# Attention feeding a mixture of experts on one core: tiles placed ahead of the gate products, constant matmuls moved, and weight splits placed later

## The chip, the core and the metric

The kernel runs on one core of a Trainium2 chip. Five engines work side by side, each through its own queue in order: TensorE (PE, with PEld for its weight loads), VectorE (DVE), ScalarE (ACT), GpSimd (POOL) and SyncE (SP), which only issues transfers. The metric is the device time of one launch in microseconds.

## The reference

The reference is two stages in float32. The first is linear attention over 8 batches, 8 heads, 576 positions and a head width of 64, with a norm per head:

```python
kv = np.einsum('bhsd,bhse->bhde', k, v)
out = np.einsum('bhsd,bhde->bhse', q, kv)
rms = np.sqrt(np.mean(out * out, axis=-1, keepdims=True) + 1e-06)
x = (out / rms * g_norm)          # 4608 tokens of 512 columns
```

The second routes every token to one of 8 experts and applies that expert's two matrices:

```python
logits = x @ w_gate;  e_idx = np.argmax(logits, axis=1)
gate_w = softmax(logits)[e_idx];  eom = sigmoid(x @ w_output_gate)
for e in range(8):
    h = np.maximum(x[e_idx == e] @ w1[e], 0.0)        # 512 -> 1024
    out[e_idx == e] = gate_w * eom[:, e] * (h @ w2[e])  # 1024 -> 512
```

## The kernel before

The program has two stages that overlap. **The attention stage** (`p1_main`, L870) goes batch by batch. `kv_part` multiplies keys with values (PSUM tile kvps, L504; copied to aug by ScalarE at L510 and to kvc by VectorE at L512). `kvT_part` transposes the result (kvTps, L521; ScalarE's copy to kvT, L523). `m_part` forms the gate products, so that logits come out of the same matmul as the attention rows (mps, L534; ScalarE's copy into aug, L536). `out_tile` (ops, L574) then makes one tile of 128 tokens from the queries and aug; it uses one of the two PSUM buffers tagged "big", as do mps and the later hps, and ScalarE empties it in three steps (L579 rows, L581 squares, L582 gate products). In batch b the tiles of batch b-1 are worked, four or five of them. The text calls the stretch from one kvps to the next a half-loop.

Every tile also advances the routing of finished groups of tiles (8, 8, 8 and 12 tiles; `route`, L605): VectorE sums squares (L595), norms, takes the maximum, counts with TensorE (rps, L709 to L716), and makes one-hot tiles la (L752; by GpSimd in the first two groups, by a mixture in the others) and rrc (L762 to L769). TensorE sums these into a table of row numbers (tblps, L782), from which VectorE makes the gather list gidx (L942 for the lead, L953 for the rest). A group's weights and norms go out as xtail (L775, written by L804).

**The expert stage** works on runs. After 24 tiles the fullest expert's first 384 tokens are taken as the *lead*, run 0; run 1 is that expert's remainder; runs 2 to 8 are the other experts. A run gathers its rows (xg, L244), scales heads (L260), transposes (tps, L284, in PSUM buffers tagged "t", emptied by L289 and L290 into a high and a low part), multiplies with the first weights (hps, L322; 3 matmuls per product of high and low parts; hT by L337 and L338) and then with the second (yps, L371). Weights arrive raw (wraw, L199) and `split` makes the high and low part: L219 on ScalarE and L222 on VectorE for the first weights, L226 and L229 for the second.

On TensorE, ScalarE, VectorE and GpSimd the order in this stage is the order in which the code is written. Two things set it. `HOOKS` and `TAIL` are strings of steps: R advances the routing, L takes a step of the lead (`lead_run`, L390), S makes one split of the lead's second weights (`lead_w2`, L405). `COLD` counts *constants* (`constant`, L482): matmuls of a tile of ones whose result nobody reads. They stand in kvps (two per piece for the first three batches), in kvTps (2), in mps (3), and as three of 512 columns after each `m_part` (cps). SP's order is set by a scheduler.

Of the kernel before, what the change touches and what calls it, by code (L numbers as in the profile page):

```python
# [69 lines left out]


HOOKS = {15: 'R', 27: 'RR', 28: 'R', 31: 'RGW', 32: 'X', 34: 'NL'}
TAIL = "QLLLLRRRSLSRRSLLRRRLSLRRSRLSLL"

WAITS = {}

# [7 lines left out]


COLD_B = 3
COLD = (2, 20, 2, 3, 3)

ROUND = 1.5 * 2.0 ** 30

# [39 lines left out]
def tiles_of(i):  # L130

    _, t0, n = RUNS[i]
    return [(t0 + k, k * P, min(P, n - k * P)) for k in range(-(-n // P))]
# [6 lines left out]
def body(ctx: ExitStack, tc: tile.TileContext, kvm, rem, qT, wg, gn, w1, w2, kc, xs, tab, out):  # L140
# [249 lines left out]
    def lead_run():  # L390

        split(0, 1, 0, SPLITS[0])
        yield
        for k in range(len(tiles_of(0))):
            stage(0, k)
            yield
        split(0, 1, 1, SPLITS[1])
        yield
        for f in range(8):
            mm1(0, f)  # L400
            if f in (0, 2):
                split(0, 1, f // 2 + 2, SPLITS[f // 2 + 2])
            yield
# [78 lines left out]
    def constant(ps, n, start=True):  # L482

        for _ in range(n):
            k = ps.shape[1] // P
            nc.tensor.matmul(ps, ones, ones.unsqueeze(1).to_broadcast([P, k, P]), start=start, stop=start)

    def kv_part(b):

# [58 lines left out]
    def out_tile(g):  # L548
# [9 lines left out]
            chunk[:] = [g, take([P, 2, DM], F32, "xrow")]  # L558
        xrow = chunk[1][:, g - chunk[0]]
        ps = ps_b.tile([P, 2, 512], F32, name="ops", tag="big")  # L560
        parts = []
        n0 = g * P
        while n0 < (g + 1) * P:
# [41 lines left out]
    def route(gi):  # L605
# [171 lines left out]
        if gi == LEAD_GROUP:  # L777
            lead_placed.append(gi)
        yield from pause(8)
        for t in range(n):  # L780
            g = g0 + t
            nc.tensor.matmul(tps, las[t], rc[:, t, 0:2], start=(g in (0, LEAD_TILES)), stop=(g in (LEAD_TILES - 1, NT - 1)))  # L782
# [87 lines left out]
    def p1_main():  # L870
        load(SPARE)
        for b in range(B):
            lim = tiles_ready(b - 1) if b else 0
            cp = kv_part(b)
            load(SPARE)
            run_out(lim)
            kvT = kvT_part(cp)
            run_out(lim)
            run_out(lim)
            m_part(b, kvT)  # L880
            constant(ps_t.tile([P, 512], F32, name="cps", tag="t"), COLD[4])
            while done_tiles < lim:
                run_out(lim)
        while done_tiles < NT:
            run_out(NT)
        for step in TAIL:
            act(step)
        while routing:
            advance()
# [321 lines left out]
```

## Time and profile before

| | us |
|---|---|
| median of 3 runs | 588.94 |
| lowest, highest | 587.86, 590.38 |
| profiled execution, whole | 591.15 |
| its span | 589.4 |
| TensorE busy | 562.4 (95%) |
| VectorE busy | 258.3 (44%) |
| mean granted clock | 0.963 |

The busy shares are averages over both stages. In the timeline a row is start, duration, engine, line, operation and tiles with the count of merged instructions, and in brackets the idle time before it with what ended that. A matmul's duration includes its passage through the array; starts of successive rows give the rate. In rows of stretches the columns are the stretch, its length, busy time and count for PE, PEld, DVE, ACT and POOL, then the granted clock (1.00 is full), the share of the transfer engines, and GB/s.

### The profile page before, as it was taken

How to read it: one execution, taken by the hardware profiler on the slowest of the kernel's cores; microseconds unless marked ns; L12 is line 12 of the kernel's file. 1: busy time of each engine (PE TensorE's matmuls, PEld its weight loads, DVE VectorE, ACT ScalarE, POOL GpSimd, SP SyncE). 2: the span in 40 equal slices, each digit the busy share in tenths (PEclk: the TensorE clock that was granted, in tenths of full speed). 3: DMA queues.
4: the chain of work that ended last, by engine and by line, in shares of the span. 5: the costliest groups of instructions: out<-in, count | busy, mean ns of one | idle time of the engine just before them, and what ended most of it. 6: DMA issues, size and time to landing. Idle time of an engine off the chain costs nothing.

```text
span 589.4 us, 10666 instructions
## 1 busy us (share of the span) xinstructions
PE 562.4 (95%) x4287; PEld 491.6 (83%) x4287; DVE 258.3 (44%) x562; ACT 223.2 (38%) x411; POOL 145.8 (25%) x150
## 2 busy tenths in 40 slices
PE   7999898869999999999999999999999999999995
PEld 4677777758798998889889987998799889889974
DVE  2136677698325556325531443244334424523410
ACT  1356555643235334323432343235234323532410
POOL 2002330401722511620172027003600540011011
PEclk9899898578999999999999999999999999999998
DMA  8999995681564622342335233524342343200001
GB/s 277 382 408 405 408 374 173 225 295 32 156 254 135 213 78 92 107 159 85 123 95 185 80 108 99 175 72 132 101 153 100 111 165 103 80 36 20 1 19 45
DMA packets 33460, 92.26 MB, mean 157 GB/s; under 512 B 8801, under 2 KB 8929, under 8 KB 33408
## 3 DMA queue, kind: packets, MB, share of 16 engines
q1 hardware_dynamic: 26672, 71.63, 34.5%
q0 software_dynamic: 6304, 19.70, 10.6%
q8 instruction: 35, 0.57, 0.4%
q10 hardware_dynamic: 432, 0.21, 0.1%
q14 instruction: 17, 0.14, 0.1%
HBM read 72.34 MB, written 19.70 MB: 156 GB/s over the span
## 4 chain that ended last, share of the span: by engine, by line
PE 79%; DMA 7%; issue 5%; DVE 4%; POOL 2%; ACT 1%; POOLq 0%; SPq 0%; DVEq 0%
PE hps L322 35%; PE yps L371 33%; PE yps L365 3%; PE tps L284 3%; DMA ld<-qT 2%; PE ops L574 2%; DMA ld<-rem 2%; PE kvps L504 2%; POOL la L752 2%; DMA ld<-kvm 2%; DMA xg<-xs,gidx 1%; DVE ss L595 1%; DMA out<-y,oidx 0%; DVE wlo L222 0%; DVE wlo L229 0%
## 5 line engine op out<-in xcount | busy, mean ns | idle before, releaser
L322 PE MATMUL hps<-xT,whi 128*128 128x256 f32 (+8 forms) x1024 | 192.7, 306 | 5.1 <-DVE hT L338 4.6
L371 PE MATMUL yps<-whi,hT 128*128 128x512 f32 (+3 forms) x592 | 195.0, 398 | 0.0
L322 PEld LDWEIGHTS hps<-xT,whi 128*128 128x128 f32 x1024 | 160.1, 191 | 7.2 <-DVE hT L338 4.2
L371 PEld LDWEIGHTS yps<-whi,hT 128*128 128x128 f32 (+3 forms) x592 | 110.1, 186 | 24.1
L322 PE MATMUL hps<-xT,wlo 128*128 128x304 f32 (+8 forms) x512 | 119.6, 305 | 0.0
L371 PE MATMUL yps<-wlo,hT 128*128 128x512 f32 (+3 forms) x296 | 115.9, 392 | 0.0
L338 DVE SCALAR_TENSOR_TENSOR hT<-hps,hT 128x512 fp32r<-128x512 f32 (+6 forms) x112 | 57.9, 518 | 124.3 <-ACT hT L337 124.3
L337 ACT ACTIVATE hT<-hps 128x512 fp32r<-128x512 f32 (+6 forms) x112 | 51.5, 460 | 144.8 <-PE hps L322 115.0
L322 PEld LDWEIGHTS hps<-xT,wlo 128*128 128x128 f32 x512 | 87.4, 191 | 0.0
L244 POOL DMA_INDIRECT xg<-xs,gidx x42 | 42.7, 1018 | 169.3 <-PE tps L284 91.8
L382 POOL DMA_INDIRECT out<-y,oidx x42 | 44.5, 1059 | 147.9 <-ACT y L381 106.6
L371 PEld LDWEIGHTS yps<-wlo,hT 128*128 128x128 f32 (+3 forms) x296 | 55.1, 186 | 11.2
L222 DVE SCALAR_TENSOR_TENSOR wlo<-wraw,gcol,whi 128x1024 fp32r<-128x1024 f32 x32 | 44.4, 1387 | 40.2 <-ACT whi L219 40.2
L381 ACT ACTIVATE y<-yps,tl 128x512 f32<-128x512 f32 (+3 forms) x37 | 25.5, 688 | 71.4 <-PE yps L371 67.6
L260 POOL TENSOR_TENSOR xg<-xg 128x512 f32<-128x512 f32 (+7 forms) x39 | 41.7, 1072 | 41.0 <-DMA xg<-xs,gidx 33.9
L289 ACT CAST xT<-tps 128x512 fp32r<-128x512 f32 (+9 forms) x45 | 23.2, 518 | 68.7 <-PE tps L284 67.1
L290 DVE TENSOR_TENSOR xT<-tps,xT 128x512 fp32r<-128x512 f32 (+9 forms) x45 | 27.1, 604 | 44.5 <-ACT xT L289 44.0
L229 DVE TENSOR_TENSOR wlo<-wraw,whi 128x1024 fp32r<-128x1024 f32 x32 | 39.2, 1224 | 14.2 <-ACT whi L226 7.1
L574 PE MATMUL ops<-aug,ld 64*128 64x80 f32 (+1 forms) x640 | 41.8, 289 | 0.6 <-issue 0.6
L574 PEld LDWEIGHTS ops<-aug,ld 64*128 64x128 f32 (+1 forms) x640 | 37.3, 194 | 5.8 <-ACT aug L536 3.0
L219 ACT ACTIVATE whi<-wraw,gcol 128x1024 fp32r<-128x1024 f32 x31 | 35.5, 1145 | 0.0
L226 ACT CAST whi<-wraw 128x1024 fp32r<-128x1024 f32 x32 | 33.3, 1041 | 1.7 <-DMA wraw<-w 1.7
(163 smaller groups left out, 400.6 us busy)
## 6 DMA issues: line engine op xcount, KB each, us to landing
wraw<-w SPq DMA_DIRECT2D x64, 512.0 KB, 3.6
ld<-kvm SPq DMA_DIRECT2D x32, 512.0 KB, 10.1
ld<-qT SPq DMA_DIRECT2D x18, 512.0 KB, 10.2
xs<-xrow SPq DMA_DIRECT2D x13, 512.0 KB, 11.6
xs<-xrow SPq DMA_DIRECT2D x2, 1280.0 KB, 15.0
ld<-rem SPq DMA_DIRECT2D x3, 512.0 KB, 10.2
xg<-xs,gidx POOLq DMA_INDIRECT x42, 3.6
out<-y,oidx POOLq DMA_INDIRECT x42, 3.1
```

The costliest lines, as they stand in the source:

```text
L219: he.activation(hi, r, AF.Copy, scale=gcol[:, 0:1])
L222: eng.scalar_tensor_tensor(out=lo, in0=r, scalar=gcol[:, 0:1], in1=hi.bitcast(F32), op0=ALU.mult, op1=ALU.subtract)
L226: he.copy(hi, r)
L229: eng.tensor_tensor(out=lo, in0=r, in1=hi.bitcast(F32), op=ALU.subtract)
L244: gathered = nc.gpsimd.indirect_dma_start(out=x[:M, :], out_offset=None, in_=rows, in_offset=bass.IndirectOffsetOnAxis(ap=gidx[:M, p, t:t ...
L260: eng.tensor_tensor(out=v, in0=v, in1=f, op=ALU.mult)
L322: nc.tensor.matmul(ps[:, j, :n], w[:, o:o + P], x[d][:, j * N:j * N + n], start=(d == 0 and k == 0), stop=(d == 3 and k == 2))
L337: nc.scalar.activation(hh, x, AF.Relu)
L338: nc.vector.scalar_tensor_tensor(out=v(h[:, l:l + n]), in0=x, scalar=0.0, in1=hh.bitcast(F32), op0=ALU.max, op1=ALU.subtract)
L371: nc.tensor.matmul(ps[:M], a, b, start=(f == 0 and k == 0), stop=(f == 7 and k == 2))
L382: i_ = nc.gpsimd.indirect_dma_start(out=out, out_offset=bass.IndirectOffsetOnAxis(ap=oidx[:M, p, t:t + 1], axis=0), in_=y[:M], in_offset=N ...
L574: nc.tensor.matmul(ps[r0:r0 + m, u, p * W:(p + 1) * W], qt[g // 2][r, p, q0:q0 + m], augs[b % 3][r, p, :], start=True, stop=True)
```

## The change

Four edits are made. In each batch but the first, two tiles now stand ahead of `kvT_part` and all other tiles of the previous batch between it and `m_part`; before it was one tile and two tiles, with the rest behind `m_part`. In the last batch one tile stays ahead of `kvT_part`, one stands between, and two come behind `m_part`. The constants in kvTps go from 2 to 1, in mps from 3 to 1, and the three of 512 columns after `m_part` go. New constants stand in the late tiles (from tile 28 on, two of 192 columns each, in a part of the tile's PSUM that the tile does not use), ahead of the lead group's table (five of 512) and ahead of each of the lead's three transposes (four of 512, in a buffer tagged "t"). And in `TAIL` the first S steps move behind later routing and lead steps, and two S at the end of the list of splits go, since there are only four splits.

```diff
-TAIL = "QLLLLRRRSLSRRSLLRRRLSLRRSRLSLL"
+TAIL = "QLLLLRRRLRRLLRRRSLSLRRSRLSLL"
...
-COLD = (2, 20, 2, 3, 3)
+COLD = (2, 20, 1, 1)
+COLD_L = (2, 5, 4)
+COLD_TILES = 28
...
         for k in range(len(tiles_of(0))):
+            constant(cold(), COLD_L[2])
             stage(0, k)
...
-            k = ps.shape[1] // P
-            nc.tensor.matmul(ps, ones, ones.unsqueeze(1).to_broadcast([P, k, P]), start=start, stop=start)
+            k = ps.shape[1] // D
+            nc.tensor.matmul(ps, ones, ones[:, 0:D].unsqueeze(1).to_broadcast([P, k, D]), start=start, stop=start)
+    def cold():
+        return ps_t.tile([P, 512], F32, name="cps", tag="t")
...
         ps = ps_b.tile([P, 2, 512], F32, name="ops", tag="big")
+        if g >= COLD_TILES:
+            constant(ps[:, 1, NP * W:512], COLD_L[0])
...
         yield from pause(8)
+        if gi == LEAD_GROUP:
+            constant(cold(), COLD_L[1])
...
             run_out(lim)
+            if b + 1 < B:
+                run_out(lim)
             kvT = kvT_part(cp)
-            run_out(lim)
-            run_out(lim)
+            while done_tiles < (lim if b + 1 < B else lim - 2):
+                run_out(lim)
             m_part(b, kvT)
-            constant(ps_t.tile([P, 512], F32, name="cps", tag="t"), COLD[4])
             while done_tiles < lim:
                 run_out(lim)
```

Line numbers after the change are 4 to 13 higher than before. How the instructions stand on TensorE in the half-loop of batch 5 (its kvps starts at 65.01 us before); repeated rows are left out. Before:

```order
L504 MATMUL kvps<-ld 64x64 x40
L574 MATMUL ops<-aug_116,ld 128x80 x8
L486 MATMUL kvTps<-ones 128x256
...
L521 MATMUL kvTps<-ident,kvc 128x128 x2
L574 MATMUL ops<-aug_116,ld 128x80 x16
L486 MATMUL mps<-ones 128x256
...
L534 MATMUL mps<-gw,kvT 64x16 x8
L486 MATMUL cps<-ones 128x512
...
L574 MATMUL ops<-aug_116,ld 128x80 x8
L504 MATMUL kvps<-ld 64x64 x40
```

and now:

```order
L511 MATMUL kvps<-ld 64x64 x40
L583 MATMUL ops<-aug_116,ld 128x80 x16
L490 LDWEIGHTS ones
L490 MATMUL kvTps<-ones 128x256
L528 MATMUL kvTps<-ident,kvc 128x128 x2
L583 MATMUL ops<-aug_116,ld 128x80 x16
L490 MATMUL mps<-ones 128x256
L541 MATMUL mps<-gw,kvT 64x16 x8
L511 MATMUL kvps<-ld 64x64 x40
```

One tile is eight rows of ops: two tiles now stand ahead of the transposes and two behind, the gate products come directly ahead of the next kvps, and cps is gone. On VectorE, from the last gate scaling of the last group to its third hT; before:

```order
L229 TENSOR_TENSOR wlo<-wraw,whi 128x1024
L338 SCALAR_TENSOR_TENSOR hT<-hps,hT 128x384
L222 SCALAR_TENSOR_TENSOR wlo<-wraw,gcol,whi 128x1024
L229 TENSOR_TENSOR wlo<-wraw,whi 128x1024
L655 TENSOR_REDUCE lg<-gp 128x12x8
...
L681 TENSOR_TENSOR ohb_120<-rsc,rsx 128x96
L229 TENSOR_TENSOR wlo<-wraw,whi 128x1024
L338 SCALAR_TENSOR_TENSOR hT<-hps,hT 128x384 x2
```

and now:

```order
L341 SCALAR_TENSOR_TENSOR hT<-hps,hT 128x384
L225 SCALAR_TENSOR_TENSOR wlo<-wraw,gcol,whi 128x1024
L664 TENSOR_REDUCE lg<-gp 128x12x8
...
L690 TENSOR_TENSOR ohb_120<-rsc,rsx 128x96
L341 SCALAR_TENSOR_TENSOR hT<-hps,hT 128x384 x2
```

Three splits of the second weights have left this place. They now stand behind the last group's table, ahead of the gather list of run 1 (VectorE, now):

```order
L784 TENSOR_TENSOR xtail<-rdn 128x12
L937 TENSOR_TENSOR t_2029<-tblps,perm 128x96
...
L941 SCALAR_TENSOR_TENSOR gl<-t_2031 128x6
L232 TENSOR_TENSOR wlo<-wraw,whi 128x1024
L341 SCALAR_TENSOR_TENSOR hT<-hps,hT 128x384
...
L965 TENSOR_TENSOR gif<-gif,gl 128x3
L969 TENSOR_TENSOR tbl<-tbl,tla 128x48
L341 SCALAR_TENSOR_TENSOR hT<-hps,hT 128x384
L966 CAST gidx<-gif 128x3
```

Between the third hT and the list there is nothing else; the left-out rows in the middle are the second and third split and the second hT. On TensorE the table's matmuls (tblps) of the last group stood behind nine yps and now stand ahead of them. On SP the lead's xtail write now stands ahead of the lead's first weight load, where it stood behind it.

## The prediction

> **What bounds the kernel now.** I read the page first, then the chain of waits, then the timelines of the engines between 30 and 150 us.
>
> ```profile
> span 589.4 us, 10666 instructions
> PE 562.4 (95%) x4287; PEld 491.6 (83%) x4287; DVE 258.3 (44%) x562; ACT 223.2 (38%) x411; POOL 145.8 (25%) x150
> ```
> ```profile
> 143.80 3.37 DMA xg<-xs,gidx
> 147.19 0.69 DVE xg L260
> ...
> 147.96 0.64 PE tps L284 x4
> ...
> 157.12 7.03 PE yps L371 x30
> 164.14 13.74 PE hps L322 x96
> 177.89 2.08 PE yps L371 x9
> 179.97 0.44 PE tps L284 x4
> ```
> The second fence is the chain of waits. From the first transposes of the remainder run (tps at 147.96) it is TensorE alone, matmul after matmul, to the last tiles. So nothing behind that point changes, and the whole question is **when tps(147.96) starts**: whatever moves it moves the end by as much. It waits for a gather whose list comes from the routing of the last group. Before it lie the attention half-loops, one per batch. Their TensorE rows:
>
> ```profile
> 41.73 2.70 PE L504 MATMUL kvps<-ld 128*64 128x64 f32 x80
> ...
> 51.60 2.63 PE L504 MATMUL kvps<-ld 128*64 128x64 f32 x77
> ...
> 65.01 3.83 PE L504 MATMUL kvps<-ld 128*64 128x64 f32 x80
> ...
> 72.96 0.49 PE L486 MATMUL mps<-ones 128*128 128x256 bf16 x3 [0.46 <-ACT gp L582]
> ...
> 73.73 0.82 PE L486 MATMUL cps<-ones 128*128 128x512 bf16 x3
> 74.48 1.12 PE L574 MATMUL ops<-aug,ld 64*128 64x80 f32 x16
> 75.54 2.63 PE L504 MATMUL kvps<-ld 128*64 128x64 f32 x77
> ...
> 87.69 4.21 PE L504 MATMUL kvps<-ld 128*64 128x64 f32 x80
> ```
> A half-loop runs from one kvps row to the next. Two of them (from 51.60 and from 75.54) hold a wait for GpSimd, which makes eight one-hot tiles one after the other:
>
> ```profile
> 58.21 5.16 POOL L752 TENSOR_SCALAR la<-ni,rlon 128x128 bf16<-128x128 f32 x8 [9.10 <-DVE rlon L731]
> 81.56 4.88 POOL L752 TENSOR_SCALAR la<-ni,rlon 128x128 bf16<-128x128 f32 x8 [18.18 <-DVE rlon L731]
> ```
> These end at 63.37 and 86.44; TensorE stands behind them in order. The others are paced by TensorE and ScalarE.
>
> **Part 1: constants out of the half-loops, tiles ahead of the gate products.** Each half-loop loses three 128x512 constants (0.75 us, from 73.73 to 74.48) and three of 128x256 (0.14 each by the row at 72.96, 0.42), so 1.17 us. The stall of 0.46 there does not vanish: the gate products now wait for the PSUM of a later tile. ScalarE's pace sets that:
>
> ```profile
> 71.08 0.46 ACT L523 COPY kvT<-kvTps 128x256 f32<-128x256 f32 x1
> 71.54 0.58 ACT L579 COPY xrow<-ops 128x512 f32<-128x512 f32 x1
> ...
> 72.68 0.66 ACT L579 COPY xrow<-ops 128x512 f32<-128x512 f32 x1
> ```
> One tile takes it 1.14. With four tiles, kvps is free to start again after one tile on TensorE (1.06, 74.48 to 75.54), three on ScalarE (3.42), its kvT copy (0.4) and the gate products (0.45): 5.3 us after the last kvps ended. Before it was 6.7 (68.84 to 75.54). A plain half-loop therefore gains **1.4**. Two lie ahead of the first GpSimd wait, and that would be 2.8, unless the loads are later:
>
> ```profile
> 34.92 4.23 SPq L479 DMA_DIRECT2D ld<-kvm x4
> 40.09 0.33 SPq L479 DMA_DIRECT2D ld<-rem x1
> ...
> ld<-rem SPq DMA_DIRECT2D x3, 512.0 KB, 10.2
> ```
> The remainder rows issued at 40.09 land 10.2 later, at 50.3, and the last fifth of kvps (0.5) can end at 50.8, where it ended at 54.2. So 3.4 is the most, and 2.8 fits. In the half-loop from 51.60 the chain kvps, VectorE, GpSimd has a fixed length, and behind it now stand a tile and the gate products (0.45) where there was a tile: 0.4 is given back. The half-loop from 65.01 gains 1.4, and the one from 75.54 gives back 0.4 again. The kvps at 87.69 starts 2.8 - 0.4 + 1.4 - 0.4 = **3.4 earlier**. Bounds: 0, if each half-loop only waits longer for the loads or GpSimd, and 5.0, if the last kvps also runs at the warm 2.63 instead of 4.21.
>
> **Part 2: constants ahead of the lead.** From the last kvps the path is VectorE's routing of the lead group, the gather, GpSimd's scaling and the transposes:
>
> ```profile
> 92.35 0.42 DVE L512 COPY kvc<-kvps 128x256 f32<-128x256 f32 x1 [2.11 <-ACT aug L510]
> ...
> 101.43 0.17 DVE L775 TENSOR_TENSOR xtail<-rdn 128x8 f32<-128x8 f32 x1
> ```
> ```profile
> 100.63 0.88 PE L782 MATMUL tblps<-rrc,la 128*128 128x96 bf16 x8 [1.67 <-DVE rrc L769]
> 101.44 8.27 PE L574 MATMUL ops<-aug,ld 64*64 64x80 f32 x96
> 110.34 2.11 PE L284 MATMUL tps<-ident,xg 128*128 128x128 f32 x8 [0.63 <-POOL xg L260]
> 113.45 1.09 PE L284 MATMUL tps<-ident,xg 128*128 128x128 f32 x4 [0.99 <-POOL xg L260]
> ```
> VectorE works 9.1 us without a gap and its order there is unchanged, so this shifts whole. The five new constants (0.25 each, 1.25) fit into the 1.67 in which TensorE waits. The sixteen of 192 columns (at most 0.14 each, two per tile, 0.28) lie beside ScalarE's 1.14 per tile: nothing; without that cover they would cost 2.2. What they may buy is the clock:
>
> ```profile
> 98.30:101.70 3.40, 1.73 (x33) 1.34 (x34) 3.37 (x16) 1.37 (x3) 0.00 (x0) 1.00 0.44 128
> 101.70:105.10 3.40, 3.40 (x56) 3.23 (x49) 3.04 (x11) 1.90 (x5) 0.29 (x1) 0.50 0.25 51
> ```
> The next to last but one number is the granted clock: after a stretch with the 1.67 gap it fell from 1.00 to 0.50, and the four transposes of 113.45 took 1.09 where 0.44 is the warm figure (179.97). Warm, the two groups of four constants between the transposes (2.0) end as the third tile's rows come: 110.34 + 0.44 + 1.0 + 0.44 + 1.0 = 113.2. Then the part **gains 0.65**. Cold, at twice the time, 110.34 + 1.1 + 2.0 + 1.1 + 2.0 = 116.5, and it **loses 3.1**. I take 0.4 gained, since the constants themselves fill the time in which the clock would come back.
>
> The Trainium skill (TensorE: Matmul & The Clock Gate, "Why this matters for your kernels") lets TensorE fall back only over idle gaps of more than about 3 us. By that rule the 1.67 gap would have been harmless and these constants buy nothing, so the sum below would be 3.9 and the time 585.0 us; the trace, with 0.50 granted behind that gap, disagrees.
>
> **Part 3: the second weights' splits later.**
>
> ```profile
> 122.36 1.22 DVE L229 TENSOR_TENSOR wlo<-wraw,whi 128x1024 fp32r<-128x1024 f32 x1
> 123.50 0.55 DVE L338 SCALAR_TENSOR_TENSOR hT<-hps,hT 128x384 fp32r<-128x384 f32 x1
> ...
> 138.19 0.27 DVE L752 TENSOR_SCALAR la<-ni,rlon 128x128 bf16<-128x128 f32 x1
> ...
> 142.89 0.16 DVE L953 CAST gidx<-gif 128x3 int32<-128x3 f32 x1
> ```
> ```profile
> 124.10 0.61 PE L322 MATMUL hps<-xT,whi 128*128 128x384 f32 x2 [2.88 <-DVE hT L338]
> 139.21 0.68 PE L782 MATMUL tblps<-rrc,la 128*128 128x96 bf16 x12
> ```
> ```profile
> 116.90:138.50 21.60, 16.49 (x77) 15.30 (x77) 20.84 (x55) 10.57 (x20) 0.00 (x0) 0.72 0.60 219
> ```
> The last fence groups VectorE's work (its third pair of numbers): it is busy for 20.84 of 21.60 us and sets the last group's routing. Three splits of 1.2 (122.36) leave that stretch, so the last one-hot tile, done at 138.46, comes 3.6 earlier. The table's matmuls (139.21) no longer stand behind nine yps: another 0.75. That is 4.35 gained up to the table's end (139.9). From there to the list (142.89) it was 3.0. Now the table's five small steps (0.2 each, as the list's 0.16), three splits (3.6), three hT (0.5 each by the row at 123.50) and two list steps (0.4) come first, 6.5: 3.5 is given back. TensorE is no cover there, since hps waits for hT, and the first yps now wait for the first of these splits. Net **0.85 gained**, of which I take 0.5, because cold hps behind the wait at 124.10 can hold back the third hT. Bounds: 0, if it does so fully, and 1.5, if the warm lead brings hT sooner.
>
> **Sum.** 3.4 + 0.4 + 0.5 = 4.3. The span 589.4 becomes 585.1. The profiled execution took 591.15 in all, the median of the three runs is 588.94, 0.5 below the span; the same 4.3 off it gives **584.6 us**.
>
> **Rivals.**
> *Slower: the half-loops go cold.* The constants taken out also kept the clock up. If it stays at 0.50 there, a kvps takes 4.21 instead of 2.63, on three more of them 4.8, and a tile 1.38 (8.27 for 96 matmuls, 16 a tile) instead of 1.06, some seventeen tiles 5.4. Against: rows 41.73 and 51.60 are warm with no constant inside. 10.2 lost against 4.3 gained: 594.8. It turns the sign once the three kvps and no tile are cold (4.8).
> *The lead's constants run cold* (the 116.5 above): part 2 is +3.1 instead of -0.4, 588.1. For it: TensorE still idles ahead of tps until GpSimd is done.
> *The half-loops only wait longer* for loads and GpSimd: part 1 is 0, 588.0. Against: loads landed well ahead from 51.60 on.
> *More than I count*: the clock stays up through the last kvps (1.6) and part 3 reaches 1.5: 582.0.
>
> **Chances.** The forecast 0.50 (its own range 582.8 to 586.5), half-loops cold 0.10, lead's constants cold 0.15, only waiting 0.12, more 0.13. The range that leaves out two in ten runs from 580.8 to 589.5. A measurement of this kernel tells about 0.5%, 2.9 us, from no change: faster than 586.0 is most of the forecast, the last rival and a little of the two in between, 0.60; within 0.5% 0.30; slower 0.10.
>
> **What would show it.** Part 1: the last kvps (87.69) starts near 84.3, and the plain half-loops are about 8 us from kvps to kvps with 2.6 inside. Part 2: a granted clock of 1.00 where 101.70 to 118 had 0.50, and the last four transposes in 0.44. Part 3: the table's matmuls end near 132, the list follows 6.5 later, and tps (147.96) starts near 143.7. A clock of 0.50 in more of the stretch from 20 to 85 us, or tps later than 147, makes the forecast wrong.

## The result, and the profile after

The changed kernel takes 597.91 us (median of 4 runs, 594.71 to 599.08); the kernel before beside it took 589.63 (587.86 to 590.38). The ratio is 1.0125, 95% interval 1.0088 to 1.0161: **1.25% slower**, where 584.6 us had been forecast. The profiled execution took 599.08 us; the head of its page:

```profile
span 597.3 us, 10632 instructions
PE 562.4 (94%) x4272; PEld 491.4 (82%) x4272; DVE 258.5 (43%) x562; ACT 222.2 (37%) x411; POOL 146.5 (25%) x150
```

TensorE is busy for the same 562.4 us, in a span that is 7.9 longer. That the sum is the same says little: in it the tiles' matmuls grew from 41.8 to 43.8 us and kvps from 27.2 to 29.8, while the constants shrank from 24.5 to 22.2 and hps from 312.3 to 308.9. The chain of waits is TensorE alone from the run's first transposes on, as before, so the place to look at is again the start of those transposes:

```profile
150.12 4.36 DMA xg<-xs,gidx
...
155.25 0.66 PE tps L287 x4
```

They start at 155.25 where they started at 147.96, 7.3 later. TensorE's timeline of the half-loops (start, duration, engine, line, operation and tiles, in brackets the idle time before):

```profile
40.57 2.70 PE L511 MATMUL kvps<-ld 128*64 128x64 f32 x80
...
49.02 2.63 PE L511 MATMUL kvps<-ld 128*64 128x64 f32 x77
...
57.57 0.60 PE L793 MATMUL tblps<-rrc,la 128*128 128x96 bf16 x3 [1.47 <-DVE rrc L778]
...
60.86 0.26 PE L793 MATMUL tblps<-rrc,la 128*128 128x96 bf16 x1 [0.32 <-POOL la L761]
61.05 2.00 PE L583 MATMUL ops<-aug,ld 64*128 64x80 f32 x16
...
63.87 4.73 PE L511 MATMUL kvps<-ld 128*64 128x64 f32 x80
68.53 3.70 PE L583 MATMUL ops<-aug,ld 64*128 64x80 f32 x32
...
77.44 3.48 PE L511 MATMUL kvps<-ld 128*64 128x64 f32 x77
...
89.50 0.22 PE L793 MATMUL tblps<-rrc,la 128*128 128x96 bf16 x1 [0.38 <-POOL la L761]
...
92.46 4.43 PE L511 MATMUL kvps<-ld 128*64 128x64 f32 x80
```

Up to the first GpSimd wait all went as forecast: the kvps of batch 4 starts at 49.02 (before 51.60). Then a tile takes 2.00 where a warm one takes 1.12, kvps 4.73, two tiles 3.70, and the last kvps starts at 92.46, 4.8 later than before (87.69). In all the traces here, behind the first 25 us, the granted clock stays at 0.50 for 3.41 us or a multiple of it (before, 64.15 to 67.56); the text calls a stretch of this length a window. The clock in windows (the third number from the right; the first pair of numbers behind the length is TensorE's busy time and count):

```profile
55.45:58.87 3.42, 1.33 (x16) 0.88 (x14) 3.31 (x12) 2.35 (x6) 3.24 (x5) 1.00 1.02 405
58.87:62.28 3.41, 2.20 (x16) 1.64 (x16) 2.75 (x10) 0.00 (x0) 1.94 (x4) 0.50 1.04 413
62.28:65.69 3.41, 3.41 (x59) 3.00 (x59) 0.00 (x0) 1.43 (x4) 0.00 (x0) 0.50 1.01 401
...
75.93:79.35 3.42, 3.42 (x61) 3.02 (x61) 1.54 (x6) 1.84 (x6) 0.00 (x0) 0.50 1.05 386
```

In the wait for GpSimd, TensorE is busy for 1.33 of 3.42 us; then 0.50 is granted for six windows, the last five of which (the first and the last of these are shown) are busy without a gap. Before, only one window behind this wait was at 0.50 (64.15 to 67.56).

Further on, the lead's transposes, and VectorE from the last group's table to the list:

```profile
118.32 1.02 PE L490 MATMUL cps<-ones 128*128 128x512 bf16 x4 [1.20 <-DVE tl L283]
119.45 0.63 PE L287 MATMUL tps<-ident,xg 128*128 128x128 f32 x4
120.54 0.90 PE L325 MATMUL hps<-xT,whi 128*128 128x384 f32 x2 [0.46 <-ACT xT L292]
...
139.75 1.24 PE L793 MATMUL tblps<-rrc,la 128*128 128x96 bf16 x12 [2.81 <-DVE rrc L778]
```
```profile
141.75 1.22 DVE L232 TENSOR_TENSOR wlo<-wraw,whi 128x1024 fp32r<-128x1024 f32 x1
...
148.74 0.56 DVE L341 SCALAR_TENSOR_TENSOR hT<-hps,hT 128x384 fp32r<-128x384 f32 x1 [2.37 <-ACT hT L340]
149.21 0.16 DVE L966 CAST gidx<-gif 128x3 int32<-128x3 f32 x1
```

So the 7.3 us add up by place: +4.8 at the last kvps, +0.8 more up to the lead's first hps (120.54 against 115.00), 4.4 back up to the table's end (140.99 against 139.89), 5.2 lost again up to the list (149.21 against 142.89), and 1.0 in the gather (4.36 against 3.37); the 0.1 that this is too much is rounding.

### The profile page after: what moved, and what is told of

Same layout as the page of the kernel before. It is cut to its first block, busy times and chain, and to the rows that moved or that the text cites. A ratio compares the mean times of both kernels' runs of the same rounds, so it can differ in the third digit from the quotient of the medians.

```text
span 597.3 us, 10632 instructions
## 1 busy us (share of the span) xinstructions
PE 562.4 (94%) x4272; PEld 491.4 (82%) x4272; DVE 258.5 (43%) x562; ACT 222.2 (37%) x411; POOL 146.5 (25%) x150
## 3 DMA queue, kind: packets, MB, share of 16 engines
q0 software_dynamic: 6304, 19.70, 10.5%
## 4 chain that ended last, share of the span: by engine, by line
PE 80%; DMA 7%; DVE 4%; ACT 2%; POOL 2%; issue 2%; SPq 0%; POOLq 0%; DVEq 0%; ACTq 0%
PE hps L325 34%; PE yps L374 32%; PE ops L583 4%; PE yps L368 3%; PE kvps L511 3%; PE tps L287 3%; DMA ld<-qT 2%; DMA ld<-rem 2%; POOL la L761 2%; DMA ld<-kvm 2%; DMA wraw<-w 1%; ACT sq L590 1%; DMA xg<-xs,gidx 1%; ACT xrow L588 1%; DVE wlo L225 1%
## 5 line engine op out<-in xcount | busy, mean ns | idle before, releaser
L325 PE MATMUL hps<-xT,whi 128*128 128x256 f32 (+8 forms) x1024 | 190.5, 303 | 3.7 <-DVE hT L341 3.3
L325 PEld LDWEIGHTS hps<-xT,whi 128*128 128x128 f32 x1024 | 158.4, 189 | 5.7 <-DVE hT L341 3.6
L325 PE MATMUL hps<-xT,wlo 128*128 128x304 f32 (+8 forms) x512 | 118.4, 303 | 0.0
L225 DVE SCALAR_TENSOR_TENSOR wlo<-wraw,gcol,whi 128x1024 fp32r<-128x1024 f32 x32 | 44.5, 1390 | 40.2 <-ACT whi L222 40.1
L293 DVE TENSOR_TENSOR xT<-tps,xT 128x512 fp32r<-128x512 f32 (+9 forms) x45 | 27.2, 605 | 46.1 <-ACT xT L292 44.7
L583 PE MATMUL ops<-aug,ld 64*128 64x80 f32 (+1 forms) x640 | 43.8, 294 | 0.9 <-ACT gp L591 0.4
L583 PEld LDWEIGHTS ops<-aug,ld 64*128 64x128 f32 (+1 forms) x640 | 38.8, 200 | 5.0 <-ACT gp L591 2.4
L511 PEld LDWEIGHTS kvps<-ld 128*64 128x64 f32 (+1 forms) x640 | 26.5, 169 | 9.6 <-DMA ld<-kvm 5.9
```

Of the source, the lines that this page charges most:

```text
L225: eng.scalar_tensor_tensor(out=lo, in0=r, scalar=gcol[:, 0:1], in1=hi.bitcast(F32), op0=ALU.mult, op1=ALU.subtract)
L325: nc.tensor.matmul(ps[:, j, :n], w[:, o:o + P], x[d][:, j * N:j * N + n], start=(d == 0 and k == 0), stop=(d == 3 and k == 2))
L511: nc.tensor.matmul(ps[u * D:(u + 1) * D, p * D:(p + 1) * D], k, v, start=(s == 0 and p == 0), stop=(s == 4 and p == NP - 1))
L583: nc.tensor.matmul(ps[r0:r0 + m, u, p * W:(p + 1) * W], qt[g // 2][r, p, q0:q0 + m], augs[b % 3][r, p, :], start=True, stop=True)
```

## The experiments

All times below are medians, each beside the kernel before on the same chip (590.84 for experiments 1 to 4, 590.49 for 5 to 8, 590.08 for 9 to 11, 590.55 for 12 and 13; the table has them in this order). The right-hand columns come from each run's profile, in us from the start of its span, and show where in the program a run gains or loses: the starts of the last kvps, of the lead's gather list, of the list of run 1, and of that run's first transposes (tps). They are of one execution each: experiments 3 and 4 have the half-loops of before, and their last kvps stands at 87.74 and 86.77.

| run | us | ratio, 95% interval | last kvps | lead's list | list | tps |
|---|---|---|---|---|---|---|
| before | | | 87.69 | 102.88 | 142.89 | 147.96 |
| changed | 597.91 | 1.0125, 1.0088 to 1.0161 | 92.46 | 108.03 | 149.21 | 155.25 |
| constants back | 600.96 | 1.0170, 1.0141 to 1.0198 | 94.75 | 109.87 | 150.81 | 157.35 |
| constants out alone | 597.82 | 1.0135, 1.0099 to 1.0171 | 91.15 | 106.33 | 145.44 | 150.54 |
| splits later alone | 592.09 | 1.0022, 1.0005 to 1.0039 | 87.74 | 101.43 | 142.07 | 148.22 |
| lead's constants alone | 591.78 | 1.0020, 0.9998 to 1.0042 | 86.77 | 101.72 | 141.22 | 146.36 |
| order alone | 600.93 | 1.0185, 1.0138 to 1.0233 | 94.39 | 109.30 | 148.66 | 153.69 |
| order, not at the waits | 591.76 | 1.0011, 0.9985 to 1.0037 | 87.50 | 102.58 | 141.68 | 146.68 |
| changed, waits filled | 591.39 | 1.0008, 0.9983 to 1.0034 | 83.55 | 97.37 | 141.82 | 147.93 |
| early half-loops only | 593.69 | 1.0042, 1.0015 to 1.0070 | 87.21 | 102.17 | 142.87 | 147.95 |
| filled, old splits | 590.69 | 1.0006, 0.9982 to 1.0029 | 84.06 | 99.41 | 141.92 | 146.91 |
| before, waits filled | 590.15 | 1.0002, 0.9978 to 1.0026 | 86.99 | 100.66 | 141.24 | 146.34 |
| filled, no constants at the lead's tps | 589.28 | 1.0000, 0.9976 to 1.0024 | 84.54 | 98.22 | 138.86 | 143.98 |
| the same, splits on GpSimd | 590.88 | 1.0003, 0.9986 to 1.0021 | 84.20 | 98.68 | 141.61 | 146.66 |
| changed, old order at the waits | 595.08 | 1.0078, 1.0051 to 1.0105 | 87.17 | 101.64 | 145.75 | 151.76 |

One thing has to be known to read the last column. From tps to the end of the span it is 441.2 to 442.4 us in ten of the fifteen profiles, and 444.1 to 445.8 in the other five (experiments 5, 6, 8, 9 and 10). In these five the run's second transposes start 5.0 behind the first, and in the ten 2.7 to 3.2. None of the edits is made behind tps; what happens there, the section on the hardware shows. A profile of the five is therefore some 2 to 4 us longer than its tps says.

**1. The constants put back.** The changed kernel, with:

```diff
-COLD = (2, 20, 1, 1)
+COLD = (2, 20, 2, 3)
...
             m_part(b, kvT)
+            constant(ps_t.tile([P, 512], F32, name="cps", tag="t"), 3)
```

> The changed kernel with the half-loops' constants put back (2 in kvTps, 3 in mps, three of 512 columns behind each m_part); the new order, the lead's constants and the later splits stay. Clock theory (the constants kept the granted clock up in the half-loops): 0.50 for at most two stretches of 3.4 us between 55 and 92 us, where the changed kernel had six in a row and two more; the last kvps starts at 86 to 88 us instead of 92.46; time 597.9 - 5 = 592 to 593 us, since the parts behind the last kvps, which put tps from +4.8 to +7.3, stay. Order theory (two tiles ahead of kvTps and all others ahead of m_part are to blame): the last kvps stays at 91 us or later, time 596 us or more.

Measured: 600.96, slower still. The theory that the constants alone explain the loss falls: with them the last kvps is at 94.75. The stretch behind the first GpSimd wait of this run:

```profile
63.36 0.26 PE L793 MATMUL tblps<-rrc,la 128*128 128x96 bf16 x1 [0.32 <-POOL la L761]
63.55 2.00 PE L583 MATMUL ops<-aug,ld 64*128 64x80 f32 x16
65.48 0.82 PE L490 MATMUL mps<-ones 128*128 128x256 bf16 x3
...
66.80 1.46 PE L490 MATMUL cps<-ones 128*128 128x512 bf16 x3
68.19 3.80 PE L511 MATMUL kvps<-ld 128*64 128x64 f32 x80
```

From the last table matmul to kvps it is 4.83 us. Before it was 1.58 (63.43 to 65.01):

```profile
58.60 0.51 PE L534 MATMUL mps<-gw,kvT 64*64 64x16 f32 x16
59.04 0.82 PE L486 MATMUL cps<-ones 128*128 128x512 bf16 x3
...
63.43 0.22 PE L782 MATMUL tblps<-rrc,la 128*128 128x96 bf16 x1 [0.36 <-POOL la L752]
63.58 1.51 PE L574 MATMUL ops<-aug,ld 64*128 64x80 f32 x16
```

There only one tile stood behind the wait, while the gate products and constants stood ahead of it and ran while GpSimd worked. Now they stand behind it, and at half the clock.

**2. The constants out, alone.** The kernel before, with:

```diff
-COLD = (2, 20, 2, 3, 3)
+COLD = (2, 20, 1, 1)
...
-            constant(ps_t.tile([P, 512], F32, name="cps", tag="t"), COLD[4])
```

> The kernel before with only the constants of the half-loops taken out (1 in kvTps, 1 in mps, none behind m_part); its order, lead and splits are unchanged. Clock theory: at least three more stretches of 3.4 us at 0.50 between 55 and 92 us than the kernel before, the last kvps at 89 to 92 us instead of 87.69, time 591 to 594 us. Prediction's theory (the constants only take time there, 1.2 us per half-loop): the last kvps at 84 to 86 us, time 587 us. Order theory: no later than before, 588 to 589 us.

Measured: 597.82, 7.0 above the kernel before, so in this order the constants are worth their time, as the clock theory had it, and more than its 591 to 594. The profile shows only part of this: tps is 2.6 later, and the profiled execution is the shortest of the four (594.27; the others took 597.11 to 600.49, at a mean granted clock of 0.938 to 0.946 against its 0.951). Its kvps of batch 6 takes 4.62 at 76.01 (2.63 before), because the window behind the stretch from 70.59 falls:

```profile
70.59:74.01 3.42, 2.55 (x49) 2.06 (x45) 3.35 (x6) 3.42 (x10) 0.00 (x0) 1.00 1.03 411
74.01:77.42 3.41, 3.34 (x42) 3.20 (x44) 2.34 (x11) 1.37 (x5) 0.00 (x0) 0.50 1.02 394
```

**3. The splits later, alone.** The kernel before, with the one line:

```diff
-TAIL = "QLLLLRRRSLSRRSLLRRRLSLRRSRLSLL"
+TAIL = "QLLLLRRRLRRLLRRRSLSLRRSRLSLL"
```

> The kernel before with only the second weights' splits placed later. Prediction's part 3: the table's matmuls end 4.35 us earlier (135.5), the list 6.5 us behind them (142), tps about 0.5 to 0.9 us earlier, time 589.0 us. List theory (what the changed kernel shows: the list comes 8.2 us behind the table, since VectorE waits there for hps that run at 0.50 after TensorE's wait for the table, and the gather takes 1.0 longer): tps (147.96) at 149 to 150, time 591 to 592 us.

Measured: 592.09, 0.2% slower. The table's matmuls come 6.2 earlier (132.99; 1.4 of it is the lead, which came earlier in this execution), but the list only 0.8:

```profile
141.60 0.56 DVE L338 SCALAR_TENSOR_TENSOR hT<-hps,hT 128x384 fp32r<-128x384 f32 x1 [1.98 <-ACT hT L337]
```

The list is 7.8 behind the table's end (134.24), against 3.0 before: three splits, and then a wait of 1.98 for an hT whose hps stand behind the second weights' matmuls. Counted from the lead's list, the list takes 40.6 where it took 40.0, and tps 46.8 where it took 45.1. The edit brings nothing by itself and costs 1.7 us up to tps in the profile; 1.1 of this lies in the gather, which the next section explains.

**4. The lead's constants, alone.** The kernel before, with:

```diff
+            constant(cold(), COLD_L[2])
             stage(0, k)
...
+        if g >= COLD_TILES:
+            constant(ps[:, 1, NP * W:512], COLD_L[0])
...
+        if gi == LEAD_GROUP:
+            constant(cold(), COLD_L[1])
```

> The kernel before with only the new constants (two in each tile from 28 on, five ahead of the lead's table, four ahead of each of the lead's transposes). Prediction's part 2: clock 1.00 from 105 us on, the third tps 0.3 to 0.65 earlier than 113.45, time 589.2 us. Cover theory (the gather sets the third tps, and the four constants ahead of it wait for a tps buffer and then stand on the path): clock 1.00, but the third tps 0.5 to 1.0 later (114 to 114.5), and the time the same or up to 0.7 us more (589.6 to 590.3).

Measured: 591.78, ratio 1.0020 with an interval that includes 1. The clock is 1.00 from 89.6 to 123.7 us in this run, as forecast, and the third transposes still start only at 113.14:

```profile
113.14 0.66 PE L287 MATMUL tps<-ident,xg 128*128 128x128 f32 x4 [0.91 <-POOL xg L263]
```

They wait for GpSimd and the gather, whatever the clock is: the constants ahead of them end at 112.23. Counted from the lead's list they come at 11.42, not at 10.57, as the cover theory had it. A warm TensorE is not what was missing there.

**5. The order, alone.** The kernel before, with the new order of tiles, kvT and gate products, and all its constants.

```diff
+            if b + 1 < B:
+                run_out(lim)
             kvT = kvT_part(cp)
-            run_out(lim)
-            run_out(lim)
+            while done_tiles < (lim if b + 1 < B else lim - 2):
+                run_out(lim)
             m_part(b, kvT)
```

> The kernel before with only the new order of tiles, kvT and gate products; all its constants, its lead and its splits stay. Order theory (behind each GpSimd wait now stand a tile, the gate products and the constants, where there was a tile): from the end of the wait to the next kvps 4.8 us, as in the run with constants back, instead of 1.6 and 1.2 before; the last kvps 6 to 7 us later (94), time 597 to 599 us, or 7 to 8 above the kernel before. Clock theory alone (only the missing constants cost time): within 1 us of the kernel before.

Measured: 600.93, 10.4 above the kernel before; the order theory had said 7 to 8. From the last table matmul behind the first wait (63.92) to kvps (68.75) it is 4.83 again. By itself the order is the largest effect of the four edits, though the profile shows only 5.7 of it up to tps; 4.0 more lie behind, with the late second transposes.

**6. The order, except at the waits.** As 5, with the old order in the half-loops of batches 4 and 6 and in the last:

```diff
-            if b + 1 < B:
+            wait = b in (4, 6, B - 1)
+            if not wait:
                 run_out(lim)
             kvT = kvT_part(cp)
-            while done_tiles < (lim if b + 1 < B else lim - 2):
+            for _ in range(2 if wait else lim - done_tiles):
                 run_out(lim)
```

> As the order alone, but the two half-loops that hold the GpSimd waits (batches 4 and 6), and the last, keep the old order. Order theory, by place: the harm is only in those two, so the last kvps starts at 87 to 88 us as before, and the time is within 1.5 us of the kernel before. Rival (the order costs in every half-loop, since ScalarE then paces the gate products): the last kvps at 90 us or later, 3 us or more slower than before.

Measured: 591.76, the same as before (ratio 1.0011). So 9 of the 10 us of the order (7.0 by tps, with late second transposes in both profiles) come from the half-loops in which TensorE waits for GpSimd, and not from ScalarE's pace in the others.

**7. The waits filled.** The changed kernel, with constants inside the two GpSimd waits:

```diff
-        if gi == LEAD_GROUP:
-            constant(cold(), COLD_L[1])
+        if gi <= LEAD_GROUP:
+            c = cold()
+            constant(c, COLD_L[1])
...
+            if gi < LEAD_GROUP and t > 2:
+                constant(c, 1)
             nc.tensor.matmul(tps, las[t], rc[:, t, 0:2], ...)
```

> The changed kernel with constants inside the GpSimd waits: five of 512 columns ahead of the tables of groups 0 and 1, and one ahead of each of the last five table matmuls of these groups, where TensorE idles 1.47 + 5 x 0.35 us. Clock theory (the idle waits take the clock down and the tiles alone don't bring it back): granted clock 1.00 from 59 to 79 us, where the changed kernel had 0.50; the tile behind the wait 1.1 instead of 2.0, kvps 2.6 instead of 4.73, four tiles 4.3 instead of 7.4; the last kvps at 85 to 88 us instead of 92.46, time 591 to 594 us. Rival (windows fall to 0.50 in spite of the filled waits, or the constants delay the table themselves): last kvps 91 us or later, time 596 us or more.

Measured: 591.39, 6.5 below the changed kernel, which was measured in another set: 1.0008 against 1.0125 of the kernel before. The granted clock is 1.00 from 59 to 92 us, the last kvps is earlier than the 85 to 88 expected, and the half-loop behind the first wait reads:

```profile
60.32 0.22 PE L796 MATMUL tblps<-rrc,la 128*128 128x96 bf16 x1
60.47 1.12 PE L583 MATMUL ops<-aug,ld 64*128 64x80 f32 x16
...
62.09 2.70 PE L511 MATMUL kvps<-ld 128*64 128x64 f32 x80
...
83.55 2.70 PE L511 MATMUL kvps<-ld 128*64 128x64 f32 x80
```

Nothing but ten matmuls in each idle wait was added, and the tile takes 1.12 instead of 2.00, kvps 2.70 instead of 4.73. The last kvps starts at 83.55, where the prediction had put it (84.3). So in the changed order the clock, taken down by the idle waits, is what turned the forecast gain of the half-loops into a loss. The time is no better than before. The lead's list comes 5.5 earlier than before, but the lead's third transposes only 2.5 (110.92, 13.55 behind the list), the list of run 1, which is 8.3 behind the table's end here (141.82 against 133.54), only 1.1, and tps not at all: the lead's constants and the later splits take it back (experiments 9 and 11).

**8. The early half-loops only.** The kernel before, with order and constants changed in batches 1 to 3 alone:

```diff
+            new = 0 < b < 4
+            if new:
+                run_out(lim)
-            kvT = kvT_part(cp)
+            kvT = kvT_part(cp, new)
...
+            if not new:
+                constant(ps_t.tile([P, 512], F32, name="cps", tag="t"), 3)
```

> The kernel before with the new order and the fewer constants in the half-loops of batches 1 to 3 alone, all of which lie ahead of the first GpSimd wait; the rest is as before. By the trace of the changed kernel the kvps of batch 4 starts at 49.0 instead of 51.6, GpSimd's one-hot tiles at 55.6 instead of 58.2, and from there on everything is 2.0 to 2.6 us earlier: time 0.3 to 0.45% below the kernel before (588.5 if that is 590.8). Rival (the shift is taken back by a wait or by a clock at 0.50 behind the first GpSimd wait, since the windows fall elsewhere): the last kvps within 1 us of 87.69, time the same.

Measured: 593.69, slower (1.0042), a miss. The kvps of batches 4 to 6 start 2.0 to 2.4 earlier, as forecast, and the one of batch 7 only 0.5. The chain of waits of this run shows what takes it back:

```profile
70.31 11.09 DMA xs<-xrow
...
81.48 0.58 ACT xrow L585
```

ScalarE empties a tile into a buffer whose earlier rows are still on their way out; that transfer lands at 81.4, 11.09 after its start. (That it is slow because it stands behind the loads, which take 10.2 to 10.5 to land, is likely and not shown.) The gap it makes then costs one more window at 0.50 (83.3 to 86.7). That explains why nothing is gained: tps is at 147.95, where it was. It does not explain a loss; what the profile has of that (2.7 of span) lies behind tps, in the late second transposes.

**9. Filled waits, old splits.** As 7, with the old `TAIL`.

> The changed kernel with filled GpSimd waits, and the second weights' splits back at their old places. There the last kvps started at 83.55, the table's matmuls at 132.34, but the list came at 141.82 only, 8.4 us behind the table's end, and the run's transposes at 147.93. List theory (the later splits stand between the table and the list, and give back what the half-loops gained): the table at 136 to 137, the list 3 us behind its end (139.5 to 140.5), tps at 144 to 145, time 0.5 to 0.7% below the kernel before. Rival (the gain is lost in the lead's gather and transposes, whatever the splits do): tps at 147 or later, time the same as before.

Measured: 590.69, the same as before, and a miss. The list is 3.0 behind the table's end again (141.92, table's end at 138.91), but the table is at 137.71: the first hps started at 115.16, not earlier than before, although the lead's list came 3.5 earlier. Two windows fell to 0.50 from 105.3 on, and TensorE's constants ahead of the first two transposes then took nearly twice their time (1.89 and 1.83; 1.03 ahead of the third):

```profile
108.00 1.89 PE L490 MATMUL cps<-ones 128*128 128x512 bf16 x4
...
114.07 0.63 PE L287 MATMUL tps<-ident,xg 128*128 128x128 f32 x4
```

GpSimd was done with the third tile's rows at 109.59, and its transposes started 4.5 later. That is the cold rival of the prediction's part 2 (it had put the same rows at 116.5 instead of 113.45).

**10. The kernel before, waits filled.** Only the constants of experiment 7, in the old order.

> The kernel before with nothing but the filled waits: five constants of 512 columns ahead of the tables of the first three groups, and one ahead of each of the last five table matmuls of groups 0 and 1. Clock theory: 1.00 in the one stretch each behind the two GpSimd waits that had 0.50 (64.15 and 88.04); the two kvps of 3.83 and 4.21 take 2.63, so the last kvps starts 1.2 earlier and the lead's list 2.5 to 3 earlier (100), time 0.3 to 0.5% below the kernel before. Rival (the loads set these half-loops, or the constants cost as much as they bring): the lead's list within 1 us of 102.88, time the same.

Measured: 590.15, no difference. In its profile the windows at 0.50 behind the two waits are gone, kvps of batch 5 and 7 take 2.70 and 2.70, and the lead's list is 2.2 earlier, tps 1.6. Then the run's second transposes start 5.0 behind the first (151.32), not 2.7 as before (150.60); what that is, the section on the hardware shows. The clock gain is there and does not reach the end.

**11. Filled waits, old splits, no constants at the lead's transposes.** As 9, without the line `constant(cold(), COLD_L[2])`.

> As the run with filled waits and the old splits, without the four constants ahead of each of the lead's three transposes. Cover theory (these stand on the path, since the third waits for the buffer of the first transposes): the third tps 0.5 to 1 us earlier than with them, time 0 to 0.1% below that run. Rival of the prediction's part 2 (they keep the clock up for the first hps): the first hps run at 0.50, and the time is 0.1 to 0.3% more than with them.

Measured: 589.28, the lowest median of all. Its third transposes start at 110.30, 3.8 earlier than in 9, on a clock of 0.50. The profiled execution is one of its shorter ones (587.37 us): tps is 4.0 earlier than in the profiled one of before, and the end 3.8. But over twelve runs the ratio is 1.0000, 0.9976 to 1.0024. So it does not beat the kernel before by anything that can be measured here.

**12. Splits on GpSimd.** As 11, with the low parts of three of the lead's second weights made by GpSimd:

```diff
-SPLITS = ['VV', 'AV', 'AV', 'AV', 'AV', 'AV', 'AV', 'AV']
+SPLITS = ['VV', 'AV', 'AV', 'AV', 'AP', 'AP', 'AP', 'AV']
```

> As the run with filled waits, old splits and no constants ahead of the lead's transposes, with the low parts of the first three of the second weights' four chunks made by GpSimd instead of VectorE (its rows show it idle from 110 to 139 us). If VectorE's 20 us without a gap is what sets the list there, three splits of 1.2 less bring the table and the list 3 to 3.5 us earlier (list at 135.5 instead of 138.86), the run's transposes at 141, and the time 0.4 to 0.6% below that run. Rival (VectorE's own two-operand rows grow while GpSimd works, as 0.69 grew to 2.05 where both scaled gathered rows; or run 1's second transposes then wait): the list less than 1.5 us earlier, the time within 0.2% of that run.

Measured: 590.88; the rival holds, and the list is 2.8 later, not earlier. GpSimd's rows and VectorE's at the same time:

```profile
113.87 2.38 POOL L232 TENSOR_TENSOR wlo<-wraw,whi 128x1024 fp32r<-128x1024 f32 x1 [4.60 <-ACT whi L229]
117.38 4.79 POOL L232 TENSOR_TENSOR wlo<-wraw,whi 128x1024 fp32r<-128x1024 f32 x2 [1.13 <-ACT whi L229]
```
```profile
114.03 2.34 DVE L640 SCALAR_TENSOR_TENSOR ru<-ry 128x96 f32<-128x96 f32 x1
...
117.57 2.29 DVE L650 TENSOR_TENSOR ru<-ru,ra 128x96 f32<-128x96 f32 x1
119.89 2.39 DVE L652 SCALAR_TENSOR_TENSOR xtail<-ru,ry 128x96 f32<-128x96 f32 x1
```

Three rows of 0.26 grew to 2.3 to 2.4: 6.2 us lost for 3.6 saved.

**13. The changed kernel, old order at the waits.** The edit of experiment 6 for batches 4 and 6, made in the changed kernel.

> The changed kernel with the old order in the two half-loops that hold the GpSimd waits (batches 4 and 6) only; constants, lead and splits stay as changed. Order theory, without constants: from the end of the GpSimd wait to the next kvps 1.2 to 2.2 us instead of 3.0 and 3.0, the last kvps at 87.5 to 90 instead of 92.46, time 593 to 596 us. If the missing constants alone set it: windows of 0.50 stay, the last kvps at 91 to 92.5, time 597 to 599 us.

Measured: 595.08, the last kvps at 87.17, both in the order theory's range or 0.3 ahead of it: the place of the gate products costs some 3 us of the 8 without any constants too. From the first wait's last table matmul to kvps it is 2.1 (61.24 to 63.36). At the second wait this run meets ScalarE's wait for outgoing rows, as in experiment 8. The rest of the loss lies behind the last kvps, which is 0.5 earlier than before, while tps is 3.8 later.

## Why the prediction was wrong, point by point

In short: the change took work out of two idle waits and put it behind them, and the forecast priced it, and all that follows, at full clock. The idle waits took the clock to half, and the half-loops behind them ran at half speed.

**What bounds the kernel** was right: TensorE alone from tps on, and the end moved with it (7.3 and 7.9).

**Part 1 is where most of it failed:** 8.2 of the 11.6 us between the forecast for tps (4.3 earlier) and the measured one (7.3 later). The forecast for the last kvps was -2.8 +0.4 -1.4 +0.4 = 3.4 earlier. Measured, by the rows shown (each line is the change of that step alone; in brackets the start of the row that ends it, before and after):

| step | forecast | measured |
|---|---|---|
| up to the first GpSimd wait | -2.8 | -2.6 (51.60 to 49.02) |
| behind the first wait, up to kvps | +0.4 | +1.4 (65.01 to 63.87) |
| half-loop of batch 5 | -1.4 | +3.0 (75.54 to 77.44) |
| half-loop of batch 6, up to the wait's end | 0 | +1.1 (86.71 to 89.72) |
| behind the second wait, up to kvps | +0.4 | +1.8 (87.69 to 92.46) |

The first line is right, and so is the gain of a plain half-loop where the clock held (40.57 to 49.02 is 8.45, where 41.73 to 51.60 was 9.87). The step that failed in the second and the last is "a tile and the gate products (0.45) where there was a tile: 0.4 is given back". It counted what was added behind the wait, at the warm price, and not what was taken from ahead of it: the gate products and constants had been TensorE's work while GpSimd made its tiles. Without them TensorE idled 1.47 and then five times 0.3 to 0.4, and that took the clock. The step that failed in the third line is "The half-loop from 65.01 gains 1.4", which priced the half-loop of batch 5 at full clock. It ran at 0.50 throughout: its kvps and its two pairs of tiles took 4.73, 3.70 and 3.71, where the warm rows are 2.70, 2.02 and 2.33 (experiment 7).

**The rival "the half-loops go cold"** named this outcome (594.8) and got a chance of 0.10. Its price was too low: it read a cold tile as 1.38 from the row at 101.44, taking 96 matmuls as six tiles, but they are five (four of 16, and one of 32 smaller ones), and a tile behind the wait took 2.00. The evidence against it, that rows 41.73 and 51.60 were warm with no constant inside, was no evidence: those half-loops come ahead of any GpSimd wait, so nothing had taken their clock. The rows that bore on it stood in the trace of before: its tiles of 101.44 were busy without a gap and stayed at 0.50 (two windows, 101.69 to 108.52). The rival had the wrong place, too. It spoke of constants taken out; experiments 1, 5, 6 and 7 show that in this order it is the idle wait, since putting the constants back behind it makes things worse (600.96) and filling the wait makes them good (591.39). Only in the old order are the constants themselves worth 7 us of the median (experiment 2).

**Part 2.** The clock came as forecast (1.00 from 106.7 to 140.8), the last four transposes took 0.63, not 0.44, and the gain of 0.4 did not come; up to the lead's first hps the part loses 0.8. The step that failed is that the constants "end as the third tile's rows come". The list-to-transposes time is 11.42 (108.03 to 119.45) where it was 10.57: the four constants ahead of the third transposes wait for a PSUM buffer that VectorE frees, and the transposes start 0.5 after GpSimd has the rows ready (118.95). The five constants ahead of the table took 2.23 at 0.50 instead of 1.25. In this run VectorE was not kept waiting by that; in experiment 9 it was, for 1.58.

**Part 3.** Up to the table's end the sum was right to a tenth (4.4 regained, 4.35 forecast), with some luck: VectorE's last one-hot tile came 3.3 earlier, not 3.6, and the table's end followed it 1.1 sooner, not 0.75. The step that failed is "6.5: 3.5 is given back". The list came 8.2 behind the table, since the third hT stands ahead of it on VectorE and waited 2.37; its hps ran cold behind TensorE's own wait of 2.81 for the table, and behind yps that waited 1.43 for a split. So 5.2 were given back and the part loses 0.8; alone it loses 0.6 up to the list and 1.3 us in the time (experiment 3). That the gather then took 1.0 longer was not in the sum. It comes with the later splits, too: VectorE's fourth split now runs just when GpSimd issues the gather.

```profile
150.08 1.22 DVE L232 TENSOR_TENSOR wlo<-wraw,whi 128x1024 fp32r<-128x1024 f32 x1
150.12 2.04 POOL L247 DMA_INDIRECT xg<-xs,gidx  x1 [31.16 <-ACT whi L229]
```

GpSimd's row took 0.98 before (at 143.80). In all five runs with the later splits (the changed kernel, 1, 3, 7 and 13) it takes 2.03 or 2.04, and tps comes 6.0 to 6.5 behind the list; in the ten others it takes 0.98 or 0.99, and tps comes 5.0 to 5.1 behind.

**Part 1 alone would not have saved the forecast.** In experiments 7 and 13 the last kvps is earlier than before, and the list then follows the lead's list by 44.5 and 44.1, where it was 40.0 before and 41.2 in the changed kernel. With the old splits it is 42.5 (experiment 9), and without the lead's constants as well 40.6 (experiment 11). Parts 2 and 3, forecast to gain 0.9, take some 4 us in these profiles, once the lead comes early.

**The idle-gap rule** of the Trainium skill (TensorE: Matmul & The Clock Gate, "Why this matters for your kernels"), which the prediction weighed against a row, disagrees with this change as well: behind gaps of 1.47 and five of 0.3 to 0.4 the clock was 0.50 for 20 us.

What stays open: why a kernel whose profiled execution is 3.8 us shorter (experiment 11) has the same median. Single executions of it spread from 587.02 to 593.70 us, those of the kernel before in the same set from 587.13 to 593.15, and only one of each was profiled. An execution whose second transposes come late, as in five of the profiles, is some 2 to 4 us longer, so the share of such executions may be the answer; no run shows it.

## What to carry to other kernels

Work that fills a wait is not free to be moved: before moving matmuls past an instruction that waits for another engine, list what ran during the wait, and price what then stands behind it at the slow clock. If idle waits can't be avoided, a few matmuls inside them cost nothing and kept the clock up here; the same matmuls behind the wait cost their full time (4.83 from the wait's last table matmul to kvps in experiment 1, 3.01 in the changed kernel, where one is left). And ask of every gain which later row has a time of its own (here a list behind splits, outgoing rows behind loads) before adding it to the sum.

## What the runs showed of the hardware

**The clock does not follow busy time alone.** In the changed kernel, five windows with TensorE busy for all of 3.41 us stayed at 0.50 (62.28 to 79.35 above). The window of experiment 2 with 2.55 busy was followed by 0.50, while these windows of the changed kernel with less kept 1.00, and so did the windows behind them:

```profile
123.72:127.13 3.41, 1.54 (x9) 1.22 (x8) 3.10 (x11) 1.52 (x2) 0.00 (x0) 1.00 1.00 369
127.13:130.55 3.42, 2.03 (x12) 2.04 (x12) 3.39 (x4) 0.00 (x0) 0.00 (x0) 1.00 1.06 396
```

The former are tiles, gate products and kvps (64x80 and 128x64 in most rows), the latter hps (128x384). That the clock counts how much of the array a matmul uses is an inference from this, and not shown. It does not settle every case either: before, one window of a tile and kvps at 0.50 was enough to bring 1.00 back,

```profile
64.15:67.56 3.41, 3.41 (x58) 3.27 (x58) 0.28 (x2) 1.37 (x3) 0.00 (x0) 0.50 1.02 408
67.56:70.97 3.41, 3.41 (x68) 3.01 (x66) 1.67 (x3) 1.40 (x4) 0.00 (x0) 1.00 1.05 413
```

and 65.69 to 69.11 in the changed kernel, again 58 matmuls of kvps and a tile, was not. What the clock goes by stays open. The Trainium skill (TensorE: Matmul & The Clock Gate, "What's actually happening") says that one busy window of about 3.4 us brings the full clock back. The changed kernel disagrees: four busy ones in a row did not (62.28 to 75.93), and only the fifth did.

**Two-operand rows of VectorE wait for GpSimd, and GpSimd for them.** In experiment 12 rows of 0.26 took 2.34, 2.29 and 2.39 while GpSimd's took 2.38; the first of them ends at 116.37, GpSimd's first at 116.25. The same was seen unplanned, in experiment 9, where VectorE scales gathered rows for the run's second transposes:

```profile
149.18 0.69 DVE L293 TENSOR_TENSOR xT<-tps,xT 128x512 fp32r<-128x512 f32 x1 [1.75 <-issue]
149.79 2.05 DVE L263 TENSOR_TENSOR xg<-xg 128x512 f32<-128x512 f32 x1
```
```profile
150.22 1.05 POOL L263 TENSOR_TENSOR xg<-xg 128x512 f32<-128x512 f32 x1
```

The scaling took 2.05 instead of 0.69, TensorE waited 2.25 for it, and the next window fell to 0.50. In experiment 10 the row is 2.12. An execution in which the two engines meet loses over 2 us at a place where the profiled one of before lost nothing: this is what stands behind the late second transposes of experiments 5, 6, 8, 9 and 10, where the row takes 2.01 to 2.13 (0.68 before). In four of them the next window falls to 0.50 as well; in experiment 8, the shortest of them behind tps, it does not. Why the engines meet is open: in experiment 9 the row ahead (149.18) starts 2.27 behind tps, where it was 1.31 before, since ScalarE's cast started 0.96 later, and for that the profile shows no cause. GpSimd's gather issue of 2.04 beside a split, shown above, is the other direction: it ends 0.86 behind the split. The Trainium skill (SBUF — State Buffer, "Who interferes with whom") says that a VectorE instruction with two inputs in SBUF contends with a GpSimd instruction that reads SBUF, and calls the ports that they share an exclusive lock; these rows agree.
